# Fused Fourier filter and GELU feed-forward on one core: one more tile by seven products, and a shifted timetable around the first batch change

## The chip, the core and the metric

The kernel runs on one core of a Trainium2 chip. A core has TensorE (PE; matmuls and, as PEld, weight loads), VectorE (DVE), ScalarE (ACT), GpSimd (POOL) and SyncE (SP; it only issues transfers here), which run their own instruction lists in order and wait for each other by semaphores. SBUF holds tiles of 128 partitions; PSUM takes the results of matmuls in eight banks of 128 x 512 fp32. The metric is the device time of one execution in microseconds (us), lower is better.

## The reference

For each of 8 batches of x (3008 x 256), a real FFT along the 3008 positions is multiplied by a complex filter per frequency and channel and transformed back; the result, 24064 rows of 256, goes through a feed-forward layer with an exact GELU:

```python
X = np.fft.rfft(x, axis=1)
Y = X * (filt_r + 1j * filt_i)[None, :, :]
y = np.fft.irfft(Y, n=3008, axis=1)          # (8, 3008, 256)
h = y.reshape(24064, 256) @ w_in             # 256 -> 2048
g = 0.5 * h * (1.0 + erf(h / sqrt(2)))
out = g @ w_out                              # 2048 -> 256
```

## The kernel before, in words

**The feed-forward.** The 24064 rows are cut into 47 tiles of 512 rows (tile 0 to 46; "the sixth tile" is tile 5). `mm1(t, jc)` computes one sixteenth of the hidden layer of a tile: two matmuls of 512 columns into a PSUM bank of the kind h (three banks), then ScalarE's GELU into g_sb. The second layer of a tile comes in two forms. The plain one, `mm2_first`, makes 64 matmuls of 256 columns into banks of the kind o (two banks) and copies the result out on VectorE (L660). The other, `mm2_seven`, treats the product as a 2 x 2 block matrix and forms seven block products in place of eight, 112 matmuls of 128 columns (L714). For it VectorE first makes three kinds of sums over g: `sums_1` in four parts (L685, into s_sb), `sums_2` in two parts (L691, into g_sb), `sums_3` in two parts (L696, into a tile that lies in the space of F); and it puts the products together in eight small instructions (L729, L731, L734, L736, L737, L740, L743 twice). The sums of the weights (w_sums) are made once. Results leave by `put_rows` (L761), most of them from GpSimd's queue.

**The filter.** Batch 0 goes through a form of its own before the main loop. Batches 1 to 7 go through four stages with small matmuls. `fold` (VectorE, L109 and L110) makes sums and differences of x; `s1` (L429) is a first transform, written to DRAM (R1) by SyncE; `r1` reads it back into b_sb; then there are three units per batch, each an `s2` (L456, one h bank and three f banks), four multiplications by the filter out of PSUM on VectorE (`s2_out`, L467), sums (`s2_sum`, L473 and L474), an `s3` (L487, one h and three f banks), and two `s3_out` (ScalarE, L325, and writes to R2 in DRAM, L497). `r2` (L505) reads back into d_sb, and `s4` (L514) makes the positions of y, group by group, evicted into the ring y_sb that mm1 reads. s4 uses a table T4a, which `table_4_all` builds on GpSimd (L410, L412) in four parts, two groups of s4 for each part. The filters reach the tile Fu by transfers within the chip (`move_filters`, L130), the second lot at slot 18 on SyncE's queue; units 1 and 2 of batch 1 need them.

**The order.** Everything after batch 0 is written out in slots, 16 per tile: slot s belongs to tile t = s // 16. In a slot the calls that `put` has entered come first, then a sixteenth of the second layer of tile t - 1, then mm1 of tile t. The scheduler is manual, so each engine's list is this order. Batch 1 begins at row 3008, inside tile 5 (rows 2560 to 3071), so s4 of its first group must come before the mm1 of that tile, and that tile has a pace of its own (`late`): in its first slots the second layer of tile 4 runs alone at 14 products a slot, and mm1 follows more densely. `put` for s4 counts back from `end`, the last allowed slot, passing over slots that `busy` has taken.

**Gates.** `gate` is a copy of one element on GpSimd (L142): what follows on GpSimd's queue waits until that element has been written. The table parts stand behind such gates.

The lines of the timetable that the change touches:

```python
s2 = (27, 41, 54) if b == 1 else ...
s3 = s2[u] + ((11, 11, 12)[u] if b == 1 else ...)
end = min(end, due - 2 if u or b > 1 else 83)
plain = (0, 1, 2)
pace = lambda i: max(16 * (i - 6) // 10, 0) if t == late else i
n = lambda i: (14 * i if i < 6 else 84 + 28 * (i - 6) // 10) if t == late else 7 * i
```

Of the kernel before, what the change touches and what calls it, by code (L numbers as in the profile page):

```python
# [782 lines left out]
def kernel(  # L783
# [10 lines left out]
    nc, B, S = tc.nc, m.B, m.S  # L794
# [124 lines left out]
    for b in range(1, B):  # L919
        hi = first(b)  # L920
        e = 4 * (b == B - 1)
        s1, n1, r1 = (4, 3.3, 17) if b == 1 else (hi - 87, 3.7, hi - 73) if b == 2 else (hi - 94 - e, 3.7, hi - 80 - e)
        s2 = (27, 41, 54) if b == 1 else (hi - 74, hi - 59, hi - 44) if e else (hi - 64 + (b == 2), hi - 48, hi - 32)
        busy.update(range(s1 - 1, s1 + int(3 * n1) + 2))
# [4 lines left out]
        for u in range(3):  # L929
            put(r1 if u < 2 else s2[0] + 1, m.r1, b, u)  # L930
            put(s2[u], m.s2, b, u)
            for i in range(4):
                put(s2[u] + 2 * i + (b == 2 and u == 0), m.s2_out, b, u, i // 2, i % 2)
            for i in range(2):
                put(s2[u] + (9 + i if 1 < b < B - 1 else 7 + 2 * i), m.s2_sum, b, 2 * u + i)
            s3 = s2[u] + ((11, 11, 12)[u] if b == 1 else 12 if e or (b, u) in ((2, 0), (B - 2, 2)) else 13)
            put(s3, m.s3, b, u)
            put(s3 + 1, m.s3_out, b, u, 1)
            busy.update(range(s2[u] - 1, s2[u] + 5), range(s3 - 1, s3 + 2))
# [6 lines left out]
    for b in range(1, B):  # L946
# [8 lines left out]
        for u in range(7, -1, -1):  # L955
            due = (b * S + GRP * u) // TCH * 16
            end = min(end, due - 2 if u or b > 1 else 83)
            if b == u == 1:
# [16 lines left out]
    put(23, m.table_u)  # L975
    put(49, m.table_4_factors, g)
    for t, slot in ((3, 67), (4, 82), (5, 98)):
        put(slot, lambda t=t: m.gate(m.st["s", t][0:1, 7, 1, 255:256]))
    parts = [(w, h) for w in range(0, HB, 8) for h in range(2)]
    for i, slot in enumerate((67, 82, 98, 105)):  # L980
        put(slot, m.table_4_all, parts[2 * i:2 * i + 2])
    put(18, m.move_filters, 2, 4)
    put(20, m.weight_sums)
    plain = (0, 1, 2)
    seven = [t for t in range(NT) if t not in plain]
# [8 lines left out]
    for s in range((NT + 1) * 16):  # L994
        t, jc = s // 16, s % 16
        for f, a in at.pop(s, ()):
            f(*a)
        pace = lambda i: max(16 * (i - 6) // 10, 0) if t == late else i
        if t - 1 in seven:
            n = lambda i: (14 * i if i < 6 else 84 + 28 * (i - 6) // 10) if t == late else 7 * i  # L1000
            m.mm2_seven(t - 1, n(jc), n(jc + 1))
# [38 lines left out]
```

## Time and profile before

| what | value |
|---|---|
| median of 3 runs | 735.47 us (734.11 to 735.9) |
| the profiled execution | 734.27 us, its span 732.5 us |
| TensorE busy | 714.5 us (98%) |
| VectorE busy | 598.4 us (82%) |
| ScalarE busy | 575.9 us (79%) |
| GpSimd busy | 287.2 us (39%) |
| granted TensorE clock | 1.00 |
| slot 48 (second layer of tile 2 begins) | 77.57 us |
| slot 64 (second layer of tile 3) | 93.38 us |
| slot 80 (second layer of tile 4) | 107.22 us |
| slot 96 begins, with an s1 | 123.54 us |

A line of the profile names the line of the kernel, the engine, the operation, output<-input, shape and count; after it come busy time and mean, or, in lists by time, start and duration at the front. Brackets give the time that the engine sat idle before, and who ended it. Where several instructions of one kind stand in one row, the duration is that of the row. Durations of matmuls are modelled and longer than the distance from one to the next. Slots are found in the list of TensorE: each is a group of L656 or L714 followed by a group of L640.

### The profile page before, as it was taken

Reading aid. Unit: us, or ns where it says so; the run is one execution under the profiler, and the core shown is the slowest. Engines: PE = TensorE matmul, PEld = TensorE weight load, DVE = VectorE, ACT = ScalarE, POOL = GpSimd, SP = SyncE. Lnnn points to the kernel's source line nnn. Section 1 sums busy time; section 2 is a strip of 40 time slices with the busy share of each in tenths; the row PEclk is TensorE's granted clock in tenths of the full one; section 3 lists DMA queues with packets and bytes.
Section 4 is the critical chain, followed back from the end, with each engine's and each line's share of the span. In section 5 each row is a group of like instructions: output and inputs, shape, how many; then the busy total and the mean of one; then the engine's idle time right before and its main releaser. Section 6 shows DMA issues by size and latency. Waiting matters only on the chain.

```text
span 732.5 us, 22075 instructions
## 1 busy us (share of the span) xinstructions
PE 714.5 (98%) x9017; PEld 505.9 (69%) x9165; DVE 598.4 (82%) x1091; ACT 575.9 (79%) x1050; POOL 287.2 (39%) x546
## 2 busy tenths in 40 slices
PE   8999999999999999999999999999999999999997
PEld 4856675666777666676777667666677767777776
DVE  8975698899878998788986999779988897775666
ACT  7997778688887888778887778877888788877773
POOL 7853377864223452135611364115531121121121
PEclk9999999999999999999999999999999999999999
DMA  9886644755355553546545455355544443311011
GB/s 157 161 178 155 155 91 115 208 123 101 88 163 147 121 109 107 164 117 130 131 104 165 112 129 123 95 151 149 111 103 136 141 117 89 110 45 44 30 59 59
DMA packets 81254, 87.72 MB, mean 120 GB/s; under 512 B 13393, under 2 KB 61137, under 8 KB 81153
## 3 DMA queue, kind: packets, MB, share of 16 engines
q0 software_dynamic: 22288, 39.50, 24.1%
q1 hardware_dynamic: 58449, 46.62, 23.7%
q8 instruction: 71, 1.16, 0.7%
q14 instruction: 30, 0.25, 0.1%
q10 hardware_dynamic: 416, 0.20, 0.1%
HBM read 54.00 MB, written 46.66 MB: 137 GB/s over the span
## 4 chain that ended last, share of the span: by engine, by line
PE 85%; DVE 5%; ACT 3%; DMA 3%; issue 2%; SPq 1%; POOL 0%; DVEq 0%; ACTq 0%; POOLq 0%
PE ps_o L714 38%; PE ps_h L640 36%; PE ps_s L514 3%; PE ps_s L429 2%; PE ps_s L487 2%; PE ps_o L656 2%; PE ps_s L456 1%; DVE s_sb L685 1%; ACT g_sb L643 1%; DMA b_sb<-R 1%; ACT y_sb L325 1%; SPq L130 1%; DMA F<-in_filt_i_dram 1%; DMA x_sb<-in_x_dram 1%; DVE p L467 1%
## 5 line engine op out<-in xcount | busy, mean ns | idle before, releaser
L643 ACT ACTIVATE g_sb<-ps_h 128x512 f16<-128x512 f32 x752 | 445.5, 602 | 138.0 <-PE ps_h L640 114.4
L640 PE MATMUL ps_h<-y_sb,w_in_sb 128*128 128x512 bf16 (+3 forms) x1456 | 414.8, 365 | 1.9 <-DVE p L467 0.8
L761 POOL DMA_DIRECT2D out_dram<-ost x231 | 131.3, 575 | 387.6 <-DVE ost L743 361.2
L714 PEld LDWEIGHTS <-g_sb 128*128 128x128 f16 x2816 | 184.5, 98 | 81.3 <-issue 14.6
L640 PEld LDWEIGHTS <-w_in_sb 128*128 128x128 bf16 x1600 | 126.4, 98 | 9.6 <-issue 2.9
L714 PE MATMUL ps_o<-w_sums,g_sb 128*128 128x128 f16 x1408 | 121.9, 219 | 1.6 <-DVE g_sb L691 0.2
L714 PE MATMUL ps_o<-w_sums,s_sb 128*128 128x128 f16 x1408 | 120.6, 219 | 1.6
L714 PEld LDWEIGHTS <-s_sb 128*128 128x128 f16 x1408 | 94.9, 98 | 36.4 <-issue 2.1
L685 DVE TENSOR_TENSOR s_sb<-g_sb 128x1024 f16<-128x1024 f16 x176 | 117.1, 696 | 0.4 <-ACT g_sb L643 0.3
L714 PE MATMUL ps_o<-w_out_sb,g_sb 128*128 128x128 f16 x1408 | 113.7, 219 | 1.8
L467 DVE TENSOR_TENSOR p<-ps_s,Fu 128x1024 bf16<-128x1024 f32 x84 | 101.5, 1216 | 9.1 <-PE ps_s L456 7.5
L101 POOL DMA_DIRECT2D x_sb<-in_x_dram x156 | 79.3, 515 | 3.1 <-issue 1.6
L714 PE MATMUL ps_o<-w_out_sb,F 128*128 128x128 f16 x704 | 61.1, 219 | 0.9
L691 DVE TENSOR_TENSOR g_sb<-s_sb,g_sb 128x1024 f16<-128x1024 f16 x88 | 60.3, 687 | 1.5
L696 DVE TENSOR_TENSOR F<-g_sb 128x1024 f16<-128x1024 f16 x88 | 61.4, 697 | 0.0
L714 PEld LDWEIGHTS <-F 128*128 128x128 f16 x704 | 47.2, 98 | 15.5 <-issue 0.8
L736 DVE TENSOR_TENSOR t_sb<-t_sb,ps_o 128x256 f32<-128x256 f32 x44 | 18.3, 417 | 39.5 <-PE ps_o L714 39.0
L514 PEld LDWEIGHTS <-d_sb 96*128 96x128 bf16 x448 | 31.3, 97 | 26.1 <-issue 1.4
L325 ACT ACTIVATE y_sb<-ps_s 128x376 bf16<-128x376 f32 x95 | 45.5, 479 | 3.2 <-PE ps_s L514 3.2
L325 ACT ACTIVATE F<-ps_s 128x512 bf16<-128x512 f32 x83 | 45.6, 609 | 0.1
L327 DVE CAST a_sb<-ps_s 128x512 bf16<-128x512 f32 x54 | 34.7, 683 | 11.3 <-PE ps_s L429 11.1
L743 DVE TENSOR_TENSOR ost<-t_sb,ps_o 128x256 f32<-128x256 f32 x86 | 32.1, 414 | 13.7 <-PE ps_o L714 13.7
(160 smaller groups left out, 592.3 us busy)
## 6 DMA issues: line engine op xcount, KB each, us to landing
out_dram<-ost POOLq DMA_DIRECT2D x127, 128.0 KB, 2.8
b_sb<-R SPq DMA_DIRECT2D x21, 512.0 KB, 4.9
R<-F SPq DMA_DIRECT2D x84, 128.0 KB, 2.4
d_sb<-R SPq DMA_DIRECT2D x56, 192.0 KB, 4.3
R<-a_sb SPq DMA_DIRECT2D x108, 96.0 KB, 2.2
x_sb<-in_x_dram POOLq DMA_DIRECT2D x48, 94.0 KB, 2.7
x_sb<-in_x_dram POOLq DMA_DIRECT2D x48, 48.0 KB, 2.8
x_sb<-in_x_dram POOLq DMA_DIRECT2D x12, 188.0 KB, 5.2
```

What stands on the lines that cost most here:

```text
L101: self.nc.gpsimd.dma_start(out=xt[64 * v + to:64 * v + to + m, h, 4 * c:4 * c + 4 * n, :], in_=xv[h][at:at + m, w:w + 4 * n, :])
L325: self.nc.scalar.activation(out=out, in_=in_, func=AF.Copy, scale=1.0 if scale is None else scale)
L327: self.nc.vector.tensor_copy(out=out, in_=in_)
L467: v(out=w[:, a], in0=ps.unsqueeze(2).to_broadcast([128, 2, 2, 256]), in1=f.unsqueeze(1).to_broadcast([128, 2, 2, 256]), op=ALU.mult)
L514: nc.tensor.matmul(ps[:, 94 * i:94 * i + 94], lhsT=d[:, (grp % 2) * 4 + i, 128 * half:128 * half + 128], rhs=self.T4a[:, 4 * grp + i, 0:2 ...
L640: nc.tensor.matmul(ps[:, o:o + n], lhsT=w[:, dc], rhs=self.ring[:, dc, off:off + n], start=(dc == 0), stop=(dc == 1))
L643: nc.scalar.activation(out=self.st["g", t][:, jc, :], in_=ps, func=AF.Gelu)
L685: self.nc.vector.tensor_tensor(out=self.st["s", t][:, i:i + 2], in0=a, in1=b, op=ALU.subtract)
L691: self.nc.vector.tensor_tensor(out=a21[:, k], in0=self.st["s", t][:, k, 0], in1=a22[:, k], op=ALU.add)
L696: self.nc.vector.tensor_tensor(out=self.s4_sb[:, k], in0=a12[:, k], in1=s2[:, k], op=ALU.subtract)
L714: nc.tensor.matmul(ps[:, (m + 1) % 2, sub, :], lhsT=a[:, i, 128 * sub:128 * sub + 128], rhs=b[:, i], start=i == 0, stop=i == 7)
L761: eng.dma_start(out=out, in_=tile_[lo - r0:lo - r0 + n])
```

## The change

Six things are changed in the timetable; no computing function is.

- Tile 2 gets its second layer by seven products (`plain` loses 2). Its eight sums are entered at slots 44 to 56, and tile 2's results leave together after the last of them.
- The units of batch 1 start at slots 26, 39 and 53 in place of 27, 41 and 54; their s3 at 37, 51 and 65 in place of 38, 52 and 66. The calls that hang on them (s2_out, s2_sum, s3_out, r1 of unit 2, two thirds of the loads of batch 2) move with them, r2 of the first part goes from slot 70 to 69.
- `end` for the first group of batch 1 is 81 in place of 83: its two s4 stand at slots 80 and 81 in place of 82 and 83. Those of the second group stay at 84 and 85.
- mm1 of tile 5 begins after three slots in place of six: 16 in 13 slots in place of 16 in 10; the second layer of tile 4 runs at 14 a slot for three slots and then has 70 products in 13 slots.
- The second part of the table stands at slot 87 in place of 82, and its gate is on a fold of batch 2 (x1, third quarter) in place of a sum of tile 4.
- `table_4_factors` stands at slot 48 in place of 49.

```diff
-        s2 = (27, 41, 54) if b == 1 else (hi - 74, hi - 59, hi - 44) if e else (hi - 64 + (b == 2), hi - 48, hi - 32)
+        s2 = (26, 39, 53) if b == 1 else (hi - 74, hi - 59, hi - 44) if e else (hi - 64 + (b == 2), hi - 48, hi - 32)
...
-            s3 = s2[u] + ((11, 11, 12)[u] if b == 1 else 12 if e or (b, u) in ((2, 0), (B - 2, 2)) else 13)
+            s3 = s2[u] + ((11, 12, 12)[u] if b == 1 else 12 if e or (b, u) in ((2, 0), (B - 2, 2)) else 13)
...
-            end = min(end, due - 2 if u or b > 1 else 83)
+            end = min(end, due - 2 if u or b > 1 else 81)
...
-    put(49, m.table_4_factors, g)
-    for t, slot in ((3, 67), (4, 82), (5, 98)):
+    put(48, m.table_4_factors, g)
+    for t, slot in ((3, 67), (5, 98)):
         put(slot, lambda t=t: m.gate(m.st["s", t][0:1, 7, 1, 255:256]))
+    put(87, lambda: m.gate(m.st["x1"][0:1, 1, 11, 0:1]))
     parts = [(w, h) for w in range(0, HB, 8) for h in range(2)]
-    for i, slot in enumerate((67, 82, 98, 105)):
+    for i, slot in enumerate((67, 87, 98, 105)):
         put(slot, m.table_4_all, parts[2 * i:2 * i + 2])
...
-    plain = (0, 1, 2)
+    plain = (0, 1)
...
-        pace = lambda i: max(16 * (i - 6) // 10, 0) if t == late else i
+        pace = lambda i: max(16 * (i - 3) // 13, 0) if t == late else i
         if t - 1 in seven:
-            n = lambda i: (14 * i if i < 6 else 84 + 28 * (i - 6) // 10) if t == late else 7 * i
+            n = lambda i: (14 * i if i < 3 else 42 + 70 * (i - 3) // 13) if t == late else 7 * i
```

## The prediction

> **What bounds the kernel now.** I read the page first (busy shares, chain), then the stretches of 5 us around the change, then each engine's list of instructions in order of time there. On the page TensorE is nearly the whole span and 85% of the chain:
>
> ```profile
> PE 714.5 (98%) x9017; PEld 505.9 (69%) x9165; DVE 598.4 (82%) x1091; ACT 575.9 (79%) x1050; POOL 287.2 (39%) x546
> PE 85%; DVE 5%; ACT 3%; DMA 3%; issue 2%; SPq 1%; POOL 0%; DVEq 0%; ACTq 0%; POOLq 0%
> L714 PEld LDWEIGHTS <-s_sb 128*128 128x128 f16 x1408 | 94.9, 98 | 36.4 <-issue 2.1
> ```
>
> A busy TensorE is not one without holes, so I count its work row by row. The stretches (us, then busy us of PE, PEld, DVE, ACT, POOL) show who could hold it up where the change lies:
>
> ```profile
> 85.00:90.00 5.00, 4.95 (x35) 3.34 (x35) 4.50 (x5) 2.98 (x5) 1.78 (x3) 1.00 0.52 135
> 90.00:95.00 5.00, 4.95 (x42) 3.33 (x41) 5.00 (x11) 3.52 (x6) 0.68 (x2) 1.00 0.00 0
> 95.00:100.00 5.00, 4.95 (x81) 3.51 (x82) 4.87 (x6) 4.68 (x10) 4.84 (x7) 1.00 0.50 131
> 105.00:110.00 5.00, 4.71 (x66) 3.69 (x64) 5.00 (x11) 2.82 (x5) 5.00 (x11) 1.00 0.60 91
> 140.00:145.00 5.00, 4.15 (x44) 2.91 (x46) 4.96 (x6) 2.50 (x5) 4.64 (x7) 1.00 0.80 234
> ```
>
> VectorE is full from 87 to 110 us; the clock is 1.00 throughout. TensorE's own list gives the prices and the holes:
>
> ```profile
> 86.43 0.60 PE L656 MATMUL ps_o<-w_out_sb,g_sb 128*128 128x256 f16 x4
> 87.30 0.60 PE L656 MATMUL ps_o<-w_out_sb,g_sb 128*128 128x256 f16 x4
> ...
> 101.46 0.55 PE L714 MATMUL ps_o<-w_sums,s_sb 128*128 128x128 f16 x7
> 102.28 0.55 PE L714 MATMUL ps_o<-w_sums,s_sb 128*128 128x128 f16 x7
> ...
> 107.22 1.76 PE L714 MATMUL ps_o<-w_out_sb,g_sb 128*128 128x128 f16 x28
> 108.81 0.33 PE L514 MATMUL ps_s<-F,d_sb 96*128 96x94 bf16 x4
> 110.00 0.51 PE L714 MATMUL ps_o<-w_sums,g_sb 128*128 128x128 f16 x6 [0.20 <-DVE g_sb L691]
> 117.69 1.02 PE L640 MATMUL ps_h<-y_sb,w_in_sb 128*128 128x512 bf16 x4 [0.30 <-DVE a_sb L327]
> ```
>
> A slot with four plain products lasts 0.87 us (86.43 to 87.30), one with seven small ones 0.82 (101.46 to 102.28). At 107.22 slot 80 begins; at 110.00 and 117.69 TensorE waits for VectorE, 0.58 us in two steps up to 110.00 (110.00 less 107.22, less 36 small products at 0.055 and one s4 of 0.2) and 0.45 at 117.69. The last view is VectorE, ScalarE and GpSimd around the change:
>
> ```profile
> 68.30 1.09 ACT L325 ACTIVATE F<-ps_s 128x512 bf16<-128x512 f32 x2
> 69.78 1.08 ACT L325 ACTIVATE F<-ps_s 128x512 bf16<-128x512 f32 x2
> 71.45 4.61 DVE L467 TENSOR_TENSOR p<-ps_s,Fu 128x1024 bf16<-128x1024 f32 x4 [1.03 <-PE ps_s L456]
> 94.32 1.75 POOL L761 DMA_DIRECT2D out_dram<-ost  x3 [5.35 <-DVE ost L660]
> 96.36 2.02 DVE L696 TENSOR_TENSOR F<-g_sb 128x1024 f16<-128x1024 f16 x1
> 101.70 0.68 DVE L696 TENSOR_TENSOR F<-g_sb 128x1024 f16<-128x1024 f16 x1
> 108.66 1.28 DVE L691 TENSOR_TENSOR g_sb<-s_sb,g_sb 128x1024 f16<-128x1024 f16 x2
> ```
>
> The same L696 takes 0.68 us, or 2.02 while GpSimd builds the table (96.2 to 103.2): that overlap is a cost of its own.
>
> **Seven products for tile 2.** TensorE: 16 slots at 0.82 in place of 0.87, -0.8 us. VectorE: eight sums at 0.60 from one start to the next (L685, L691, L696) are 4.8; the recombination is 0.34 (L729), 0.78 (L731, L734), 1.11 (L736 to L740) and 0.72 (L743 twice), 2.95; two copies (L660) at 0.60 go. Net +6.55 us. Between 76 and 87 us VectorE has 6.2 us of waits (1.27, 2.97, 1.45, 0.50): the cover is about used up, and what is left over is late at tile 3 and 4. Tile 2's output also leaves in one piece: six transfers (L761) on GpSimd's queue after the last sum, at 0.58 us (1.75 for three), 3.5 us, in front of the first table part; before, three stood there.
>
> Here the Trainium skill speaks against the change: its page TensorE: Matmul & The Clock Gate, section Back-to-back issue gap, gives about 81 ns for one matmul of 128 columns in a stream of weight loads and matmuls. The rows have 0.385 us for seven in a slot (0.82 less two 512-column ones at 0.217), 55 ns each, and 57 in the run of 28 at 107.22 (1.59 us to the next row), so the trace disagrees. By an estimate from that page 112 of them would cost 9.1 us where the rows give 6.1, and the sum would be 3 us worse.
>
> **Units of batch 1 one or two slots earlier.** Their work on TensorE is the same; what matters is what is ready. Unit 0 at slot 26 reaches TensorE at 57.5; its b_sb was written by 57.1 (landing events of the trace): no wait. Unit 1 at slot 39 follows its predecessor's s3 (slot 37) by two slots. In the rows the s3 at 67.63 has its last two evictions end at 70.86, 3.2 us later; the s2 now comes 2.4 us after its s3 (as 83.93 after 81.52), needs the last bank for its second half 0.35 in, and loses 0.5 us (bounds 0 and 0.8: unit 2's s2 at 83.93, in the same position with one eviction on VectorE, lost 0.2). Its multiplications (L467) cannot start before the filters are in Fu, whose last transfer lands at 70.8: 70.85 in place of 71.45. The order on SyncE's queue is the same as before: unit 2's read of b_sb (slot 27) still stands behind the filter transfers and goes out near 72, for use at 83; the writes to R2 (L497) and the read of d_sb (slot 69) follow their evictions. GpSimd's loads of x move a slot or two with the units and meet nothing.
>
> **VectorE's list from there.** 70.85, four L467, two L660 by 0.60, three sums, four L473/L474 at 0.34, three more sums: L729 ends at 82.0, in time for every reader (TensorE needs the second-half sums in slot 52, at 82.5; the last is done at 81.6). It then waits for unit 2's s2 (83.7). From 83.7 the list is 4.61 (L467), 1.2 (L696), 0.78, 1.11, 1.36 (L473/L474), 1.8 (L685), 0.72 (L743), then 1.8 for tile 3's last sums: 97.1, where it was 95.9. TensorE is at slot 64 at 93.1 (slot 48 at 77.57 + 0.5, then 15.81 - 0.8) in place of 93.38. Slot 65's s3 needs the sums of unit 2, done at 94.05, when TensorE is at 93.9 with its first half still to do: no wait (up to 0.5 if the list is half a microsecond later).
>
> **First table part and slot 80.** GpSimd: L743 at 95.1, six L761 to 98.6, the part itself 7.1 us (96.07 to 103.23 in the rows): done at 105.9. s4 of batch 1 now stands at slot 80, which TensorE reaches at 106.9 (107.22 - 0.35): 1 us to spare. d_sb landed at 104.1 and comes earlier.
>
> **Tile 4's sums.** VectorE goes on from 97.1 with the same 13 us of work as before and the same overlap with the table, only later: L743 of tile 3 at 108.1 to 108.7 (was 107.3 to 108.05), L691 done at 109.9 to 110.5 (was 109.9). TensorE with two s4 and 36 products from 106.9 would be there at 109.3 and waits till then, about 0.9 us in place of 0.58; it has one s4 (0.2) more behind it than before.
>
> **Three slots' delay.** No work changes. The sixteen mm1 spread over 13 slots, 0.85 us each, with 0.6 us of GELU per 1.06 us rather than per 0.83, so the 0.45 at 117.69 should go. From that point to slot 96: 76 small ones 4.2, 32 mm1 at 0.217 6.9, two s4 0.4, two s1 1.1, 0.2 of smaller steps: 12.8, so 122.7 to 123.3 where slot 96 began at 123.54. VectorE has 11.6 us of work there.
>
> **Second table part at slot 87.** In the rows it began only at 114.49 (behind loads and output); its new gate is a fold at about 114.7, and with the queue ahead of it GpSimd starts near 117 and ends at 124; its first reader is slot 108, near 134. Nothing, either way; bounds +-0.3 from whom of VectorE it meets.
>
> **Sum.** -0.8 (products) + 0.5 (unit 1) = -0.3 by slot 64; +0.3 - 0.2 at tile 4; -0.45 in tile 5, some of it eaten by later sums: -0.25 to -0.85 at slot 96, middle -0.5. After that the timetable is unchanged. The profiled execution took 734.27 (span 732.5 and 1.8 around), 1.2 under the median of 735.47; against the median, 735.0. About 0.3%, 2.2 us, is what a measurement here can tell from no change.
>
> **Rivals.** *More gain:* VectorE keeps up, the waits at 39 and at tile 4 vanish too (-1.4 to -2.0), and the 0.85 us hole in 140:145 shrinks, since VectorE has caught up by then. For it: the list has only 1.3 us of lag at 97. Against: it was full from 87 on. -1.4 to -3.1, typically -2.3: 733.2. *Slower:* VectorE's list is late by more than I count (L696 at 2.02 and L109 at 1.47 show how a sum can double beside GpSimd), so L743, the six L761 and the first table part slip, and s4 at slot 80 stops TensorE in order. It decides from 1 us of slip; each further one is paid in full, and tile 4's sums with it: a slip of 3.5 gives +2.5, 737.9 to 738. For it: the part's end and slot 80 are 1 us apart, where before they had 5.6 (103.2 to 108.8). Against: the waits in VectorE's list absorb lateness. *Weight loads in the open:* each small product has its own load, 98 ns in the page's row; were it not hidden behind the product before, tile 2 would pay 112 x (98 - 55) ns = 4.8 us more: +4.3, 739.8. The slots of tile 3 (0.82) speak against it. The rule of 81 ns from TensorE: Matmul & The Clock Gate stands beside this one.
>
> **How the numbers follow.** Forecast 0.55, its own range -1.9 to +1.5 (all bounds together); more gain 0.23, of it 0.18 beyond 2.2 us; slower 0.19, of it 0.17 beyond; weight loads 0.03. Faster 0.18, same 0.62, slower 0.20. The range takes in the forecast and most of both neighbours: -2.7 to +2.6, 732.8 to 738.1.
>
> **What would show it.** L714 in slots 48 to 63 at 0.82 a slot; s2 of unit 1 stretched to over 1 us near 69; no wait of s4 at slot 80 for GpSimd (one of over 1 us makes it slower); TensorE's wait for L691 near 109 to 110; none for L327 between slots 83 and 96; slot 96 near 123. Wrong it would be most of all if VectorE ended tile 3's last sums after 98 us, or if the stretch 140:145 changed.

## The result, and the profile after

The changed kernel takes 735.93 us (median of 22 runs, 734.76 to 737.94); the kernel before, run beside it, 734.58 (22 runs, 734.11 to 735.9). The ratio is 1.0015, interval 1.0009 to 1.0021: slower by about 1.1 us, where the forecast was 0.5 us faster. The move is small, but it is a move, and it went the other way. The profiled execution took 734.76 us, span 732.9; it is the fastest of its 22, so it has to be read beside other profiles of the same kernel (below).

The page of the changed kernel, the lines that answer to those shown of before (a group of L714 loads is found by its operand; s_sb is the one shown before):

```profile
PE 714.0 (97%) x9064; PEld 505.9 (69%) x9213; DVE 603.6 (82%) x1105; ACT 576.4 (79%) x1050; POOL 285.9 (39%) x546
PE 88%; DVE 3%; DMA 3%; POOL 2%; issue 2%; ACT 1%; DVEq 0%; POOLq 0%; ACTq 0%
L714 PEld LDWEIGHTS <-s_sb 128*128 128x128 f16 x1440 | 97.4, 98 | 38.8 <-issue 2.5
```

TensorE's busy time fell by 0.5 us and VectorE's rose by 5.2; TensorE is still nearly the whole span. Three of the stretches of 5 us shown before (us, busy us of PE, PEld, DVE, ACT, POOL, then clock, DMA share, GB/s):

```profile
95.00:100.00 5.00, 4.95 (x56) 3.54 (x55) 4.93 (x8) 4.61 (x10) 4.84 (x8) 1.00 0.60 169
105.00:110.00 5.00, 4.26 (x59) 3.38 (x58) 4.96 (x11) 2.84 (x6) 5.00 (x10) 1.00 0.43 59
140.00:145.00 5.00, 4.50 (x75) 3.23 (x77) 4.96 (x7) 2.36 (x5) 4.86 (x8) 1.00 0.82 223
```

The new hole is in 105:110: 4.26 us of TensorE where there were 4.71. TensorE's own list by time shows it, and the places that the prediction named:

```profile
68.82 0.64 PE L456 MATMUL ps_s<-b_sb,T2p 64*32 64x256 bf16 x17
69.69 0.41 PE L456 MATMUL ps_s<-b_sb,T2p 64*32 64x256 bf16 x15 [0.22 <-ACT F L325]
70.03 0.61 PE L656 MATMUL ps_o<-w_out_sb,g_sb 128*128 128x256 f16 x4
...
86.45 0.55 PE L714 MATMUL ps_o<-w_sums,s_sb 128*128 128x128 f16 x7
86.84 0.59 PE L640 MATMUL ps_h<-y_sb,w_in_sb 128*128 128x512 bf16 x2
87.27 0.55 PE L714 MATMUL ps_o<-w_sums,s_sb 128*128 128x128 f16 x7
...
106.86 0.33 PE L514 MATMUL ps_s<-F,d_sb 96*128 96x94 bf16 x4
...
107.98 0.28 PE L714 MATMUL ps_o<-w_out_sb,g_sb 128*128 128x128 f16 x2
108.94 1.07 PE L714 MATMUL ps_o<-w_out_sb,g_sb 128*128 128x128 f16 x16 [0.68 <-DVE ost L743]
110.15 0.40 PE L714 MATMUL ps_o<-w_sums,g_sb 128*128 128x128 f16 x4
110.75 0.79 PE L714 MATMUL ps_o<-w_sums,g_sb 128*128 128x128 f16 x11 [0.20 <-DVE g_sb L691]
...
123.67 0.63 PE L429 MATMUL ps_s<-x_sb,T1s 47*64 47x512 bf16 x8
```

A slot of tile 2 lasts 0.82 us (86.45 to 87.27), as forecast. Unit 1's s2 at 68.82 is broken in two; slot 80 begins at 106.86 with an s4 that waits for nothing; then TensorE stops in tile 4's second layer (two of the stops stand in brackets); and no wait for L327 stands between 110.75 and slot 96 at 123.67. VectorE and GpSimd around it:

```profile
69.75 1.23 DVE L467 TENSOR_TENSOR p<-ps_s,Fu 128x1024 bf16<-128x1024 f32 x1 [5.28 <-ACT F L325]
83.67 1.23 DVE L467 TENSOR_TENSOR p<-ps_s,Fu 128x1024 bf16<-128x1024 f32 x1 [1.41 <-PE ps_s L456]
96.43 0.69 DVE L691 TENSOR_TENSOR g_sb<-s_sb,g_sb 128x1024 f16<-128x1024 f16 x1
99.32 2.13 DVE L110 TENSOR_TENSOR x_sb<-x_sb 111x1024 bf16<-111x1024 bf16 x1
108.14 0.74 DVE L743 TENSOR_TENSOR ost<-t_sb,ps_o 128x256 f32<-128x256 f32 x2
109.41 1.28 DVE L691 TENSOR_TENSOR g_sb<-s_sb,g_sb 128x1024 f16<-128x1024 f16 x2
95.16 3.47 POOL L761 DMA_DIRECT2D out_dram<-ost  x6 [15.96 <-DVE ost L743]
104.83 1.32 POOL L412 TENSOR_TENSOR F<-tmp_sb 96x376 bf16<-96x376 f32 x1
```

Tile 3's last sum ends at 97.1 and the first table part at 106.1 (forecast 97.1 and 105.9).

**Where the time went.** Executions reach tile 2 at different times: the three profiles of the changed kernel by -0.36, +0.23 and +0.23 us against the profile of before. The only slot of the change ahead of it, unit 0 at 26, meets no wait in them. So I take ScalarE's list, the start of the first GELU (L643) of each tile, as the difference to the kernel before less the difference at tile 2 (63.46 us in the profile of before). The column "behind L691" is the same difference for TensorE's first product after its wait for L691 in tile 4 (110.00 in the profile of before). All in us, one profile each:

| kernel | at tile 2 | tile 4 | behind L691 | tile 6 | tile 8 | tile 28 | tile 30 | tile 46 |
|---|---|---|---|---|---|---|---|---|
| before, second profile | +0.02 | 0.00 | 0.00 | +0.01 | +0.01 | +0.01 | +0.01 | +0.02 |
| changed | -0.36 | -0.01 | +1.11 | +0.48 | +0.64 | +0.64 | +0.64 | +0.66 |
| changed, second profile (again) | +0.23 | -0.01 | +1.12 | +0.49 | +0.67 | +0.67 | +1.28 | +1.30 |
| changed, third profile (again_2) | +0.23 | -0.01 | +1.12 | +0.49 | +0.68 | +0.68 | +1.32 | +1.34 |
| delay_only | +0.04 | 0.00 | 0.00 | -0.62 | -0.75 | -0.75 | -0.75 | -0.75 |
| delay6 | -0.17 | -0.01 | +1.12 | +1.18 | +1.17 | +1.18 | +1.60 | +1.60 |
| seven_only | +0.14 | -0.53 | +0.84 | +2.81 | +2.68 | +2.69 | +3.64 | +3.66 |
| plain2 | -0.01 | +0.64 | +0.64 | +0.02 | -0.11 | -0.11 | -0.10 | -0.11 |
| units_back | +0.18 | -0.53 | +0.83 | +0.21 | +0.36 | +0.37 | +0.37 | +0.37 |
| unit41 | +0.19 | +0.29 | +1.42 | +0.80 | +0.97 | +0.98 | +1.78 | +1.77 |
| pool_sums | +0.70 | +0.97 | +1.42 | +0.80 | +0.97 | +0.98 | +1.16 | +1.16 |
| pool_sums_ub | +0.91 | +4.06 | +5.42 | +4.79 | +4.95 | +4.95 | +5.01 | +5.00 |
| after_phase | +0.78 | +0.49 | +1.55 | +0.93 | +1.09 | +1.09 | +1.09 | +1.11 |
| before_phase | +0.69 | 0.00 | 0.00 | 0.00 | +0.01 | +0.01 | +0.01 | +0.01 |

In the ten profiles of kernels with the three slots' delay, tile 6 stands 0.62 or 0.63 below the column before it, from whatever tile 4 was: what TensorE won or lost ahead of L691 does not reach tile 6 by itself, only the end of L691 does.

The loss of the changed kernel has three parts: about 0.5 us in tiles 4 and 5 (tile 4 to 6), 0.17 near 144 us (tile 7), and in two of its three profiles another 0.6 us between tiles 28 and 30, near 460 us, far behind everything that was changed. After that nothing moves.

### The profile page after: what moved, and what is told of

Read it like the earlier page. It is cut to its first block, busy times and chain, and to the rows that moved or that the text cites. A ratio compares the mean times of both kernels' runs of the same rounds, so it can differ in the third digit from the quotient of the medians.

```text
span 732.9 us, 22185 instructions
## 1 busy us (share of the span) xinstructions
PE 714.0 (97%) x9064; PEld 505.9 (69%) x9213; DVE 603.6 (82%) x1105; ACT 576.4 (79%) x1050; POOL 285.9 (39%) x546
## 3 DMA queue, kind: packets, MB, share of 16 engines
q8 instruction: 72, 1.18, 0.7%
## 4 chain that ended last, share of the span: by engine, by line
PE 88%; DVE 3%; DMA 3%; POOL 2%; issue 2%; ACT 1%; DVEq 0%; POOLq 0%; ACTq 0%
PE ps_o L714 40%; PE ps_h L640 37%; PE ps_s L514 3%; DMA x_sb<-in_x_dram 3%; PE ps_s L429 2%; PE ps_s L487 2%; PE ps_s L456 1%; DVE s_sb L685 1%; ACT g_sb L643 1%; PE ps_c L587 1%; POOL T2p L348 1%; PE ps_o L656 1%; PE ps_c L565 0%; POOL x_sb L101 0%; POOL x_sb L92 0%
## 5 line engine op out<-in xcount | busy, mean ns | idle before, releaser
L643 ACT ACTIVATE g_sb<-ps_h 128x512 f16<-128x512 f32 x752 | 446.4, 601 | 141.3 <-PE ps_h L640 115.0
L640 PE MATMUL ps_h<-y_sb,w_in_sb 128*128 128x512 bf16 (+3 forms) x1455 | 415.1, 365 | 1.1 <-ACT g_sb L643 0.3
L761 POOL DMA_DIRECT2D out_dram<-ost x231 | 131.3, 575 | 393.9 <-DVE ost L743 377.1
L714 PEld LDWEIGHTS <-g_sb 128*128 128x128 f16 x2880 | 188.6, 98 | 83.7 <-issue 15.0
L640 PEld LDWEIGHTS <-w_in_sb 128*128 128x128 bf16 x1600 | 125.6, 98 | 7.6 <-issue 1.9
L714 PE MATMUL ps_o<-w_sums,g_sb 128*128 128x128 f16 x1440 | 124.5, 219 | 1.9 <-DVE g_sb L691 0.2
L714 PE MATMUL ps_o<-w_sums,s_sb 128*128 128x128 f16 x1440 | 124.0, 219 | 1.6
L714 PEld LDWEIGHTS <-s_sb 128*128 128x128 f16 x1440 | 97.4, 98 | 38.8 <-issue 2.5
L685 DVE TENSOR_TENSOR s_sb<-g_sb 128x1024 f16<-128x1024 f16 x180 | 119.7, 695 | 0.4 <-ACT g_sb L643 0.3
L714 PE MATMUL ps_o<-w_out_sb,g_sb 128*128 128x128 f16 x1440 | 116.5, 219 | 2.6 <-DVE ost L743 0.7
L467 DVE TENSOR_TENSOR p<-ps_s,Fu 128x1024 bf16<-128x1024 f32 x84 | 101.8, 1217 | 12.6 <-PE ps_s L456 5.7
L691 DVE TENSOR_TENSOR g_sb<-s_sb,g_sb 128x1024 f16<-128x1024 f16 x90 | 61.7, 687 | 1.5
L714 PE MATMUL ps_o<-w_out_sb,F 128*128 128x128 f16 x720 | 62.0, 219 | 0.9
L696 DVE TENSOR_TENSOR F<-g_sb 128x1024 f16<-128x1024 f16 x90 | 61.4, 682 | 0.0
L714 PEld LDWEIGHTS <-F 128*128 128x128 f16 x720 | 48.2, 98 | 15.1 <-issue 0.4
L327 DVE CAST a_sb<-ps_s 128x512 bf16<-128x512 f32 x54 | 34.7, 684 | 12.0 <-PE ps_s L429 11.7
L743 DVE TENSOR_TENSOR ost<-t_sb,ps_o 128x256 f32<-128x256 f32 x88 | 32.9, 414 | 13.7 <-PE ps_o L714 13.7
```

The lines of the kernel that those rows point to most:

```text
L327: self.nc.vector.tensor_copy(out=out, in_=in_)
L467: v(out=w[:, a], in0=ps.unsqueeze(2).to_broadcast([128, 2, 2, 256]), in1=f.unsqueeze(1).to_broadcast([128, 2, 2, 256]), op=ALU.mult)
L640: nc.tensor.matmul(ps[:, o:o + n], lhsT=w[:, dc], rhs=self.ring[:, dc, off:off + n], start=(dc == 0), stop=(dc == 1))
L643: nc.scalar.activation(out=self.st["g", t][:, jc, :], in_=ps, func=AF.Gelu)
L685: self.nc.vector.tensor_tensor(out=self.st["s", t][:, i:i + 2], in0=a, in1=b, op=ALU.subtract)
L691: self.nc.vector.tensor_tensor(out=a21[:, k], in0=self.st["s", t][:, k, 0], in1=a22[:, k], op=ALU.add)
```

## The experiments

Medians and ratios to the kernel before, run on the same chip (22 runs of the changed kernel, 5 of pool_sums_ub, 11 of each other):

| kernel | what it has of the change | median us (lowest to highest) | ratio [interval] |
|---|---|---|---|
| changed | all | 735.93 (734.76 to 737.94) | 1.0015 [1.0009, 1.0021] |
| again | all | 735.64 (734.98 to 737.61) | 1.0014 [1.0005, 1.0023] |
| delay_only | delay and table part | 733.95 (733.66 to 734.58) | 0.9987 [0.9979, 0.9996] |
| delay6 | seven products, units | 736.75 (735.6 to 737.4) | 1.0026 [1.0017, 1.0034] |
| seven_only | seven products | 735.9 (734.77 to 738.15) | 1.0014 [1.0005, 1.0023] |
| plain2 | units, delay and table part | 735.04 (734.47 to 736.31) | 1.0002 [0.9993, 1.0011] |
| units_back | seven products, delay and table part | 735.1 (734.62 to 735.79) | 1.0004 [0.9995, 1.0013] |
| unit41 | all, unit 1 at slot 41 | 736.29 (735.21 to 737.11) | 1.0018 [1.0009, 1.0027] |
| pool_sums | all, four sums of tile 2 on GpSimd | 735.53 (734.59 to 736.4) | 1.0006 [0.9997, 1.0015] |
| pool_sums_ub | the same, units back | 739.78 (738.75 to 740.48) | 1.0064 [1.0052, 1.0077] |
| after_phase | all, 160 instructions more on TensorE | 736.51 (735.15 to 738.67) | 1.0022 [1.0012, 1.0032] |
| before_phase | none, 96 instructions more on TensorE | 734.59 (734.3 to 735.01) | 0.9996 [0.9988, 1.0005] |

The sixth item of the change, `table_4_factors` at slot 48, is in all of them but delay_only, seven_only and before_phase; no run takes it alone.

**again, before_again, again_2: the same two kernels once more.** No edit.

> The changed kernel once more, for a second profile. In the first one the parts add up to +0.65 us from slot 26 on (+0.65 at unit 1's s2, -0.65 over tile 2, +0.5 over tiles 4 and 5, +0.16 near 144), while the medians are 1.35 apart. Theory A (VectorE's list, late at tile 4 through the sums of tile 2): +1.35 in the times, and a profile of a more usual execution shows the wait for L743 and L691 at slots 81 and 82 longer than the 0.7 and 0.5 us seen. Theory B (the first table part comes too late for s4 at slot 80): the same time, but the extra is a wait of the L514 at slot 80 for GpSimd's L412. Theory C (unit 1 two slots early): the extra lies near 69 us, at the L456.

> The kernel before, unchanged, for a second profile. It tells whether the wait of about 0.4 to 0.6 us of s4 for d_sb near 460 us, which shows in some profiles of the kernels with the seven products, also comes in the kernel before. If that wait is a matter of chance in every kernel, it may show here and can explain none of the difference; if it hangs on the seven products, TensorE's rows near 460 us show no wait for d_sb here, as in the first profile of the kernel before. Time 734.2 to 735.5 us.

> The changed kernel, unchanged, for a third profile. Wait of s4 for d_sb near 460 us: none in the first profile, 0.6 us in the second. If it is a matter of chance it may or may not come here; up to 150 us the profile should stand 0.6 to 0.7 us behind the profile of the kernel before from the same start, as the two others did. Time 735.0 to 736.5 us.

The result stands: 1.0014. The two further profiles of the changed kernel agree with each other and with the first to 0.04 us up to tile 28, once the start is taken off; the second of before lies on the first. The wait near 460 us came in both new profiles of the changed kernel (0.45 and 0.48 us in TensorE's list, 0.6 in the marks), not in the first, and in neither of the kernel before. None of the three theories had the place of the extra: the waits for L743 and L691 are no longer than in the first profile (0.69 and 0.21 us in again), the s4 at slot 80 waits for nothing, and the s2 near 69 us is broken as in the first.

**delay_only: the three slots' delay, s4 at 80 and 81 and the table part at 87, nothing else.**

```diff
-            end = min(end, due - 2 if u or b > 1 else 83)
+            end = min(end, due - 2 if u or b > 1 else 81)
...
-    for t, slot in ((3, 67), (4, 82), (5, 98)):
+    for t, slot in ((3, 67), (5, 98)):
...
+    put(87, lambda: m.gate(m.st["x1"][0:1, 1, 11, 0:1]))
...
-    for i, slot in enumerate((67, 82, 98, 105)):
+    for i, slot in enumerate((67, 87, 98, 105)):
...
-        pace = lambda i: max(16 * (i - 6) // 10, 0) if t == late else i
+        pace = lambda i: max(16 * (i - 3) // 13, 0) if t == late else i
...
-            n = lambda i: (14 * i if i < 6 else 84 + 28 * (i - 6) // 10) if t == late else 7 * i
+            n = lambda i: (14 * i if i < 3 else 42 + 70 * (i - 3) // 13) if t == late else 7 * i
```

> The kernel before with only the three slots' delay, s4 at slots 80 and 81, and the second table part at 87; tile 2 plain, units at 27, 41, 54. Theory A: VectorE is not late, so the spread of mm1 gives its 0.45 us and the wait of 0.58 at tile 4 stays or shrinks: -0.4 to -0.8. Theory B: the first table part ends at 103.2 as before, s4 at 107.2 does not wait: -0.4 too. Theory C: -0.4. If it is slower than before instead, the delay itself costs, and none of the three is the cause.

0.9 us faster than before (2.0 less than the changed kernel), and the fastest of all kernels here. TensorE's list of delay_only:

```profile
107.25 0.33 PE L514 MATMUL ps_s<-F,d_sb 96*128 96x94 bf16 x4
...
108.21 0.33 PE L514 MATMUL ps_s<-F,d_sb 96*128 96x94 bf16 x4
108.38 1.17 PE L714 MATMUL ps_o<-w_out_sb,g_sb 128*128 128x128 f16 x18
...
110.04 0.79 PE L714 MATMUL ps_o<-w_sums,g_sb 128*128 128x128 f16 x11 [0.21 <-DVE g_sb L691]
...
122.96 0.63 PE L429 MATMUL ps_s<-x_sb,T1s 47*64 47x512 bf16 x8
```

With VectorE on its old timetable tile 4's products run through: no wait for L743, the one for L691 ends at 110.04 (110.00 before), and the second s4 of the group fits into the time that was waited anyway. From there to slot 96 it takes 12.92 us (110.04 to 122.96), as in the changed kernel (110.75 to 123.67), where before it took 13.54 (110.00 to 123.54). The 0.62 is the whole difference at tile 6. The delay does what it was said to do and somewhat more; the slowdown is not in it.

**delay6: the changed kernel with the delay and the table part undone.** The same diff backwards, on the changed kernel.

> The changed kernel with tile 5's delay back at six slots, s4 of the first group at slots 82 and 83, the second table part at 82; tile 2 by seven products and the units at 26, 39, 53 stay. Theory A: the wait for L743 and L691 in tile 4 stays and the 0.45 us at the s1 of tile 5 comes back: +1.5 to +2 us against the kernel before. Theory B: s4 has 1.7 us more in hand, the extra goes: +0.3 to +0.7. Theory C: no difference to the changed kernel beyond the 0.45 in tile 5: +1.5 to +1.8, with the loss near 69 us.

736.75, 0.8 to 1.1 us worse than the changed kernel. The chain of waits agrees: L743 1.0 and L327 0.4. So the delay is worth about 0.9 with or without the rest, and the other two parts together cost about 2.

**seven_only: tile 2 by seven products, nothing else.**

```diff
-    plain = (0, 1, 2)
+    plain = (0, 1)
```

> The kernel before with only tile 2 by seven products; units, delay and table as before. Theory A: the saving of 0.65 to 0.8 us at slot 64 is lost again at tile 4, where VectorE is 1 to 2 us late: 0 to +1 us. Theory B: s4 at slot 82 does not wait: -0.6. Theory C: -0.6, since nothing is lost near 69 us.

735.9, 1.0 us worse than before. The profiled execution was the slowest of its 11 (738.15 us, span 736.3), so its largest wait is not that of the others. TensorE's and GpSimd's lists:

```profile
109.17 0.84 PE L714 MATMUL ps_o<-w_out_sb,g_sb 128*128 128x128 f16 x12 [1.23 <-DVE ost L743]
120.64 1.02 PE L640 MATMUL ps_h<-y_sb,w_in_sb 128*128 128x512 bf16 x4 [2.27 <-DVE a_sb L327]
117.23 1.60 POOL L410 TENSOR_TENSOR tmp_sb<-t_sb 96x376 f32<-96x376 f32 x2
```

The second table part, at slot 82 here, begins at 117.23 among the folds of VectorE, and L327 comes 2.3 us late for TensorE. That the old slot is to blame is not shown: delay6 has the seven products and the old slot too, and waits 0.35 us for L327 (118.70). VectorE here also waited 0.98 us at 115.56 for an earlier transfer of results. The 1.23 before it is the wait for L743 again, without any change to the units or to tile 5: it belongs to the seven products. The products behind L691 begin 0.84 late, which is near the 1.0 of the median.

**plain2: the changed kernel with tile 2 plain.** `plain = (0, 1, 2)`.

> The changed kernel with tile 2 plain again: units at 26, 39, 53, delay of three slots and the second table part at 87 stay. If the parts add up (delay -0.9; unit 1's s2 +0.65, the 0.85 between the two earlier runs): -0.1 to 0 us against the kernel before, so 0.8 to 1.2 under the changed kernel, and no wait for L743 at slot 81. If VectorE's lag at tile 4 is not from tile 2's sums but from the units' new places, L743 is waited for here too and it stays at +0.5 or more.

735.04, 0.6 to 0.9 less than the changed kernel. The wait for L743 is gone; what is left among TensorE's waits from 55 to 150 us:

```profile
PE ps_h L640 <- DVE p L467: 0.7, 1, 0.7
PE ps_s L456 <- ACT F L325: 0.2, 1, 0.2
PE ps_o L714 <- DVE g_sb L691: 0.2, 1, 0.2
```

In the marks it stands 0.64 behind at tile 4, all of it unit 1's s2, and delay and table then gain 0.62. Against the changed kernel this separates the seven products: they gain 0.65 by tile 4 (+0.64 to -0.01; 0.53 in seven_only and units_back) and lose 1.11 from tile 4 to 6 (-0.62 to +0.49).

**units_back: the changed kernel with the units at 27, 41 and 54.**

```diff
-        s2 = (26, 39, 53) if b == 1 else ...
+        s2 = (27, 41, 54) if b == 1 else ...
...
-            s3 = s2[u] + ((11, 12, 12)[u] if b == 1 else ...
+            s3 = s2[u] + ((11, 11, 12)[u] if b == 1 else ...
```

> The changed kernel with the units of batch 1 back at slots 27, 41, 54 (s3 at 38, 52, 66): seven products for tile 2, delay of three slots, second table part at 87. Theory A: seven products cost +1.06 alone and the delay gives -0.9 to -1.1, so 0 to +0.2 us; the wait for L743 at slot 81 is as long as in the changed kernel or up to 0.5 longer, because VectorE's list starts 0.6 us later. If unit 1's early s2 costs nothing in the end, it is +1.2 like the changed kernel.

735.1: 0.5 to 0.8 less than the changed kernel in the medians, 0.3 in the marks up to tile 28. The split s2 is gone, TensorE reaches slot 64 earlier (-0.53 at tile 4), and half of that is given back at L743, for which it now waits 0.9 us. Against delay_only, which differs by the seven products and by `table_4_factors` one slot later, it stands 1.15 us higher in the medians and 1.12 in the marks (tile 46): the products' price, measured twice. The slot of `table_4_factors` leaves nothing by tile 4, where seven_only, without the move, stands at -0.53 as well.

**unit41: the changed kernel with only unit 1 back, at slot 41, its s3 at 51.**

```diff
-        s2 = (26, 39, 53) if b == 1 else ...
+        s2 = (26, 41, 53) if b == 1 else ...
...
-            s3 = s2[u] + ((11, 12, 12)[u] if b == 1 else ...
+            s3 = s2[u] + ((11, 10, 12)[u] if b == 1 else ...
```

> The changed kernel with unit 1 of batch 1 back at slot 41 and its s3 at 51 as it was; units 0 and 2 stay one slot earlier (26 and 53), the seven products and the three slots' delay stay. Theory: what the moved units cost is the second transform of unit 1 at slot 39, which comes two slots after the s3 of unit 0 and while Fu still fills, so it goes here: TensorE's rows near 69 us show no stretched s2 of 32 matmuls, the time falls by 0.6 to 1.0 us against the changed kernel, to a ratio of 0.9998 to 1.0006 against the kernel before. Rival: any earlier unit (26 or 53) costs it through VectorE's list, then it stays within 0.3 us of the changed kernel, ratio 1.0012 to 1.0020.

The theory got its mechanism and missed its price. TensorE's list of unit41:

```profile
71.11 0.63 PE L456 MATMUL ps_s<-b_sb,T2p 64*32 64x256 bf16 x32
...
80.70 0.42 PE L487 MATMUL ps_s<-p,U 32*64 32x256 bf16 x16
81.65 0.65 PE L487 MATMUL ps_s<-p,U 32*64 32x256 bf16 x16 [0.52 <-DVE p L473]
```

The s2 runs whole again, 0.57 us to the next row as before the change (the split one took 1.21, 68.82 to 70.03). But its s3, ten slots on, now stops for the sums L473 that stand behind tile 2's sums in VectorE's list, and the kernel is no faster: 736.29. In units_back the s3 stands at slot 52 and has no such wait. With tile 2's sums in VectorE's list, an s2 at slot 41 leaves the s3 a wait at 51 and none at 52; other places were not run.

**pool_sums and pool_sums_ub: is it VectorE's load?** Four of tile 2's eight sums go to GpSimd: two of `sums_1`, entered at slots 38 and 42, and both of `sums_3`. pool_sums_ub has the units back at 27, 41, 54 besides.

```diff
-        self.nc.vector.tensor_tensor(out=self.st["s", t][:, i:i + 2], in0=a, in1=b, op=ALU.subtract)
+        eng = self.nc.gpsimd if t == 2 and i < 4 else self.nc.vector
+        eng.tensor_tensor(out=self.st["s", t][:, i:i + 2], in0=a, in1=b, op=ALU.subtract)
...
-        self.nc.vector.tensor_tensor(out=self.s4_sb[:, k], in0=a12[:, k], in1=s2[:, k], op=ALU.subtract)
+        eng = self.nc.gpsimd if t == 2 else self.nc.vector
+        eng.tensor_tensor(out=self.s4_sb[:, k], in0=a12[:, k], in1=s2[:, k], op=ALU.subtract)
...
-            put(16 * t + s, m.sums_1, t, 2 * i)
+            put((38, 42)[i] if t == 2 and i < 2 else 16 * t + s, m.sums_1, t, 2 * i)
```

> The changed kernel with four of tile 2's eight sums (the first two of sums_1, entered at slots 38 and 42, and both of sums_3) on GpSimd, which stands idle from 78 to 95 us: 2.4 us less on VectorE, the same products on TensorE. Theory A: the wait for L743 (0.7) and most of that for L691 (0.5) go, -0.8 to -1.2 us against the changed kernel: 0 to +0.4 against before. If the lag at tile 4 comes from the folds and the table part beside them and not from tile 2's sums, no gain, and it stays at +1.1 to +1.4; if GpSimd's sums slow VectorE's L467 beside them, it is slower than that.

> The same four sums on GpSimd, and the units of batch 1 back at slots 27, 41, 54: what the runs so far would point to. Delay -0.9, tile 2's products -0.65 with VectorE no longer late, no loss at unit 1: -1.0 to -1.6 us against the kernel before. If the gains of seven products cannot be had at all beside VectorE's load, 0.

In pool_sums the wait for L743 is gone, but not because VectorE is earlier: counted from the same start its last L743 (L745 in this kernel) ends at 109.56 us, where it ended at 109.24 in the changed kernel. TensorE comes a microsecond later (+0.97 at tile 4), since it waits 1.1 us at L456 for L327, and the products behind L691 begin at +1.42 in place of +1.11. The median is 0.1 to 0.4 us under the changed kernel's (0.6 by the ratios), the expected gain of 0.8 to 1.2 is missed, and the run took nothing off VectorE's lateness, so it does not decide the question that it was made for. pool_sums_ub is 4 us worse than either, and its lists say why (DVE, POOL, PE; in this kernel L692 is the sum called L691 elsewhere, L698 is L696):

```profile
80.84 2.49 DVE L692 TENSOR_TENSOR g_sb<-s_sb,g_sb 128x1024 f16<-128x1024 f16 x1
83.25 0.41 DVE L473 TENSOR_TENSOR p<-p 128x512 bf16<-128x512 bf16 x1
83.59 2.33 DVE L474 TENSOR_TENSOR p<-p 128x512 bf16<-128x512 bf16 x1
80.57 2.21 POOL L698 TENSOR_TENSOR F<-g_sb 128x1024 f16<-128x1024 f16 x1
83.47 2.17 POOL L698 TENSOR_TENSOR F<-g_sb 128x1024 f16<-128x1024 f16 x1 [0.69 <-ACT g_sb L643]
83.72 0.32 PE L487 MATMUL ps_s<-p,U 32*64 32x256 bf16 x8 [1.06 <-DVE p L473]
85.97 0.32 PE L487 MATMUL ps_s<-p,U 32*64 32x256 bf16 x8 [1.94 <-DVE p L474]
```

A VectorE sum that starts while GpSimd makes one ends 0.3 to 0.6 us after GpSimd's end: L474 takes 2.33 us in place of 0.41, L692 2.49 in place of 0.69. pool_sums has the same: an L473 of 2.49 us and an L692 of 2.50. GpSimd at 2.2 us a sum takes no load off VectorE while both run. The granted clock of pool_sums_ub was 0.995 to 0.998, but its marks do not move after tile 8 (+4.95 to +5.00), so the loss is in these waits. The page SBUF — State Buffer of the Trainium skill, section Who interferes with whom, states that a VectorE instruction with two inputs in SBUF contends with a GpSimd instruction that reads SBUF, that the shared ports are an exclusive lock, and that the order of issue decides who is blocked. The rows agree; they fit L110 beside the first table part too (99.32 above, 2.13 us; 0.69 at 114.35 us of the same profile, where GpSimd issues loads).

**after_phase and before_phase: the wait near 460 us.** What is late there is d_sb, read back from R2 after its last write has landed. In the trace's records of DMA packets there is one of 16,384 bytes of the kind "instruction" on queue 8 on average for every 256 matmuls and weight loads (72 of them on the page for 18,426 matmuls and weight loads, the count in again_2, 71 for 18,330 in before_again). Seven products for tile 2 add 96 instructions, and the later packets come earlier, in again by 2.6 us in the middle, counted from the same start (3.6 in before_phase below). In the table, packets of queue 8 from 446 us on, the last write to R2 (issue and landing) and TensorE's wait:

| profile | code packet starts at | last R2 write: issued, landed, us | wait of s4 for d_sb |
|---|---|---|---|
| before | 446.83 and 455.49 | 451.05, 454.11: 3.06 | none |
| before_again | 446.19 and 455.62 | 451.08, 454.14: 3.06 | none |
| plain2 | 446.50 and 455.49 | 450.93, 453.97: 3.04 | none |
| changed | 452.67 | 451.33, 455.20: 3.87 | none |
| units_back | 452.90 | 451.60, 455.35: 3.75 | none |
| again | 453.32 | 451.95, 455.90: 3.95 | 0.5 |
| again_2 | 453.25 | 451.96, 456.28: 4.32 | 0.5 |
| unit41 | 453.53 | 452.22, 456.36: 4.14 | 0.6 |

The profiles left out agree: 3.06 us in delay_only, with packets at 445.84 and 454.79, and 3.91 to 4.25 in delay6, seven_only, pool_sums and pool_sums_ub, each with a packet between issue and landing. A late landing does not always cost TensorE a wait.

Two more kernels move the packets without touching any slot: warm-up matmuls of 512 columns, all before 30 us, are cut into smaller ones with as many columns in all. after_phase adds 160 instructions, which with the 96 makes one full packet; before_phase adds 96.

```diff
         for i in range(n):
-            self.nc.tensor.matmul(ps, lhsT=self.ones[:, 0:128], rhs=self.ones, start=True, stop=True)
+            self.warmed = getattr(self, "warmed", -1) + 1
+            k = 4 if self.warmed >= 10 else 2 if self.warmed >= 5 else 1
+            for o in range(0, 512, 512 // k):
+                self.nc.tensor.matmul(ps[:, o:o + 512 // k], lhsT=self.ones[:, 0:128], rhs=self.ones[:, o:o + 512 // k], start=True, stop=True)
```

(In before_phase the choice of k is `4 if self.warmed >= 19 else 1`.)

> The changed kernel with 160 more instructions on TensorE, all before 30 us: 25 of the warm-up matmuls of 512 columns are cut into four of 128, five into two of 256, so that no column is added. With the 96 that tile 2's seven products add this makes 256. In the profiles one transfer of 16,384 bytes of the kind instruction comes for every 256 matmuls and weight loads; with the seven products one falls on 452.7 to 454.0 us, between the writes to R2 and their landing, in the kernel before it falls on 446.8 and 455.5. Theory: this transfer holds up the last write to R2 (3.75 to 4.3 us to landing in place of 3.05) and through it s4 of batch 5. Then here it falls on 446 to 447 and 455 to 456 us again, the last R2 write at 452 us lands after 3.0 to 3.2 us, TensorE has no wait for d_sb near 461 us, and the time falls by 0.4 to 0.6 us against the changed kernel, to a ratio of 1.0006 to 1.0010. Rival: the slow landing comes from being late at that place, wherever the code transfers fall: then landing 3.75 us or more, the wait of 0.5 us is there, ratio 1.0012 to 1.0020.

> The kernel before with 96 more instructions on TensorE, all before 30 us: 16 of the warm-up matmuls of 512 columns are cut into four of 128, no column is added. Theory: the transfer of code that came at 446.8 us comes at 452 to 453 us, as with the seven products, the last write to R2 near 451.05 us lands after 3.7 us or more in place of 3.06, s4 near 460 us waits for d_sb by 0 to 0.5 us, and the time rises by 0 to 0.5 us, ratio 1.0000 to 1.0007. Rival: no effect of the place of the code transfers: landing 3.05 us, ratio 0.9996 to 1.0004.

The place of the packet decides. The DMA view of again, from the issue of the last R2 write (451.9 to 455.9 us), and the landing times of its last two R2 writes:

```profile
q8 instruction: 1, 0.02, 1.7%
out_dram<-ost POOLq DMA_DIRECT2D x3, 128.0 KB, 3.6
...
DMA to landing us min/median/max: 2.2/3.1/4.0
```

The same view of after_phase (452.9 to 456.9 us), which has no line of q8 there, and its last R2 write:

```profile
out_dram<-ost POOLq DMA_DIRECT2D x3, 128.0 KB, 2.5
...
DMA to landing us min/median/max: 3.1/3.1/3.1
```

And before_phase (451.7 to 455.7 us), where the kernel before now has the packet:

```profile
q8 instruction: 1, 0.02, 1.4%
out_dram<-ost POOLq DMA_DIRECT2D x3, 128.0 KB, 3.5
...
DMA to landing us min/median/max: 2.3/3.1/3.9
```

In after_phase the packets came at 448.93 and 457.53, the write landed after 3.08 us and TensorE had no wait near 460 (tile 28 to 30: +1.09 to +1.09 in the marks). In before_phase the packet came at 453.19 and the write took 3.91, as with the seven products; the wait did not come, so there the kernel before has some slack. The times, though, went otherwise than the theory said: after_phase is not 0.5 us faster than the changed kernel but 0.6 to 0.9 slower. Its profile shows a new wait, of unit 2's s2 at slot 53, behind an eviction that itself waited for an earlier write to R2 (DVE's and PE's lists; the lines of this kernel are 3 higher):

```profile
84.51 0.69 DVE L330 CAST F<-ps_s 128x512 bf16<-128x512 f32 x1 [1.63 <-DMA R<-F]
85.25 0.41 PE L459 MATMUL ps_s<-b_sb,T2p 64*32 64x256 bf16 x16 [0.59 <-DVE F L330]
```

A code packet falls at 81.65 in this profile, where again has its own at 82.98; that it makes this write late too was not tried. The wait costs 0.5 us by tile 4; still the marks end 0.2 us below those of again (+1.11 to +1.30). What makes the profiled time longer is that it reached tile 2 0.55 us later (+0.78 to +0.23). Whether the cut warm-up matmuls make the start late is not shown; before_phase started +0.69 late, and its median is no longer than before. That the packet lengthens the R2 write near 452 is shown, in both directions; that it costs the changed kernel 0.6 us there is shown as far as one place goes; that another place for the packets would make the kernel faster is not.

## Why the prediction was wrong

**Seven products for tile 2.** On TensorE right: -0.53 to -0.65 in the marks for -0.8, slots of 0.82 us. Right too in VectorE's list: tile 3's last sums ended at 97.1, the six L761 ran from 95.16 to 98.63 (forecast 95.1 to 98.6); since this execution came 0.36 us early to tile 2, that is 0.3 to 0.4 later than forecast from the same start. The rule of 81 ns for a matmul of 128 columns (the Trainium skill, TensorE: Matmul & The Clock Gate, section Back-to-back issue gap) did not hold here: seven of them take 0.39 us (86.45 to 86.84), 56 ns each. The step's end, that waits cover all but a little of the 6.55 us, is what failed, at the next step but two.

**Units one or two slots earlier.** The mechanism was right and the size in its bounds: unit 1's s2 lost 0.64 us (1.21 less 0.57) for 0.5. Fu was there earlier than said (first L467 at 69.75 and 70.57 in two profiles, forecast 70.85), which is worth nothing, since VectorE then waits for unit 2's s2 until 83.67 (forecast 83.7). Unit 0 met no wait in any of the three profiles, as said. What the step left out is that nothing pays the 0.64 back. In the medians the units cost more than in the marks (plain2 less delay_only: 1.1 against 0.64; the intervals are about 0.7 wide each way), and that rest stays open.

**VectorE's list, first table part.** Right: no wait of the s3 in slot 65, the part done at 106.1 for 105.9, s4 at slot 80 at 106.86 for 106.9 without a wait (0.7 us to spare for 1). The rival *slower* had this place, and it did not happen there.

**Tile 4's sums.** This is the step that failed. It said that TensorE would wait for L691 about 0.9 us in place of 0.58, until 109.9 to 110.5. The products behind L691 began at 110.75. From slot 80 to there TensorE took 3.89 us in place of 2.78; its own work is 36 products at 0.055 and two s4 at 0.2, 2.4 us, so it stood 1.5 us, in three steps, the first behind L743 from near 108.1, a wait that the step did not have. The term that was mis-sized is VectorE's work between tile 3's last sum (its second L691) and the end of tile 4's L691, put at 13 us "as before". The row of before with that last sum (the one with L691 stands in the prediction):

```profile
95.26 0.69 DVE L691 TENSOR_TENSOR g_sb<-s_sb,g_sb 128x1024 f16<-128x1024 f16 x1
```

It ends at 95.95 and L691 at 109.94, the 95.9 and 109.9 of the prediction: 14.0 us apart, with no wait of VectorE over 0.1 us between them. With 14.0 in place of 13 its own sum gives 111.1; measured is 110.69, 111.05 from the same start (0.36 added). The lag of 1.2 us that VectorE was to have at 97.1 was thereby taken to shrink to between 0 and 0.6 by L691. From the same start it was 1.6 at tile 3's last sum (97.1 against 95.9) and still 1.1 at the end of L691 (110.69 against 109.94). Those 1.1 us are the whole loss from tile 4 to 6 that plain2 sets apart: the 0.65 that tile 2 gained on TensorE was waited away here, and 0.5 more. The sign that the prediction set for itself, tile 3's last sums after 98 us, did not come: up to there the list was near its forecast, and it was the shrinking behind it that was wrong.

**Three slots' delay.** Right, and in itself a gain that was undersized: 12.92 us to slot 96 for 12.8, the wait for L327 gone; alone it is worth 0.62 by slot 96, 0.75 at tile 8 and 0.9 [0.3, 1.5] in the medians (0.0013 of 734.9, with its interval).

**Second table part.** Nothing, as said: it ran from 116.41 to 121.8, and TensorE has no wait there.

**Sum.** At slot 96 the forecast was -0.25 to -0.85, the marks say +0.5: a difference of 1.0 to its middle, of which 0.15 is tile 2's smaller gain, 0.15 unit 1's larger loss, 0.6 tile 4's sums (3.89 us from slot 80 to the products behind L691, where 106.9 to the middle of 109.9 to 110.5 was forecast) and 0.1 tile 5 (12.92 for 12.8). Two terms were not in the sum at all: 0.17 near 144 us, where L640 waits 0.98 us for L467 in again (0.80 before) and, in the first profile, 0.27 us after 0.63 for b_sb at 140.19, though the timetable there is unchanged, the cause of which stays open; and the 0.6 near 460, from the place of TensorE's code packets. With them the profile of again stands 1.3 us behind, which is what the medians show (1.1 to 1.35). The three parts add: -0.9 for delay and table, about +1.1 for the seven products and, by the medians, +0.5 to +1.1 for the units. The median of 735.47 that the forecast started from was of three runs; more runs put it at 734.6 to 734.9. With 22 runs of each the interval of the result is 0.9 us wide in all, much finer than the 2.2 us that the prediction took for the least that can be told.

## What to carry to other kernels

Work put on an engine that is not the bound is not paid where it is done but where the bound next waits for that engine: carry its lateness forward, from row to row, to that wait (here from 97 us to 110), and do not let it shrink on the way unless a wait in its list takes it in. A change of several parts deserves a forecast, and a run, for each part: here one part alone beat the kernel before by 0.9 us and the changed one by 2.0, and the others gave it back. And a change in the number of instructions moves the code packets of all that follows, so a few tenths of a microsecond can come or go at places that nobody touched (here 0.5 us near 460).

## What the runs showed of the hardware

- TensorE's code comes in DMA packets of 16,384 bytes, one for 256 matmuls and loads, about every 10 us, most 0.9 to 1.7 us long. One that fell between the issue and the landing of the last R2 write near 452 us held it up by 0.7 to 1.3 us (3.05 to between 3.75 and 4.32), and transfers of results beside it by about 1.0 (2.5 to 3.6 in after_phase and again). The Trainium skill, page Runtime: NRT & Kernel Launch, section Instruction fetch mechanics, gives the blocks of 16 KiB and 256 instructions on a queue of the sequencer's own, with a cost that is mostly hidden. The size agrees; the cost shown here is in the other transfers.
- A sum on VectorE that started beside a sum on GpSimd lasted until 0.3 to 0.6 us after that one was done: 0.41 became 2.33 us, 0.69 became 2.49.
- Executions reached tile 2, at 63 us, up to 1.3 us apart (-0.36 to +0.91 over all kernels here, -0.36 to +0.70 where the code up to there is that of the changed kernel). The three profiles of the changed kernel agree to 0.04 us up to tile 28 once that is subtracted, much more finely than medians do.
